# Attention and two MLPs on one core: the attention's steps for all head pairs from one written-out list, masks moved as 16 rows, another order of the first MLP's units

## The chip, the core and the metric

The kernel runs on one core of a Trainium2 chip. The core has TensorE (PE, matmuls into the PSUM banks), VectorE (DVE), ScalarE (ACT), GpSimd (POOL) and SyncE (SP), which issues the DMAs here. Each engine takes its instructions from a list of its own, in order, and waits at an instruction until the semaphores of what it reads or overwrites are there. The metric is the device time of the program in microseconds.

## What is computed

Three layers in a row, in fp32. First an attention in which a query sees only the keys that fall into the same cluster (2 batches, 8 heads, 768 tokens, 64 columns per head, 16 clusters):

```
q_assign = np.argmax(np.einsum('bhsd,hcd->bhsc', q_n, c_n), axis=-1)
k_assign = np.argmax(np.einsum('bhsd,hcd->bhsc', k_n, c_n), axis=-1)
mask = q_assign[:, :, :, None] == k_assign[:, :, None, :]
scores = np.where(mask, scale * np.matmul(q, k.transpose(0, 1, 3, 2)), -1000000000.0)
attn = exp(scores - max(scores)); attn = attn / (sum(attn) + 1e-09)
x = np.matmul(attn, v)                                # then [1536 tokens, 512]
x = ((x @ w1) * (x @ w2)) @ w3 @ w_out                # d_ff 1024
out = (sigmoid(x @ w_gate) * (x @ w_val)) @ w_out2    # d_ff 1536
```

## The kernel before

Every fp32 operand of a product is split into a rounded upper half and the rest (`hi`, `lo`), and a product is three matmuls (`mm3`, lines 65 to 67). The eight matrices of the MLPs arrive as 64-bit words and are converted on the chip (`f64_steps`): a load, and then ScalarE, GpSimd and VectorE in turn.

The attention goes by pairs of heads (`pr`, 0 to 7; four pairs are a batch). A pair has two heads (`e`) of three blocks of 256 queries, so there are 48 blocks `i`, and each block has two score tiles `j`. For a block:

- `scores(j)`: four matmuls into a PSUM tile of `ps_s` (two buffers). The operands `QH`, `KH` hold the 64 upper halves and, in rows 64 and up, the one-hot code of the query's cluster and a penalty for each key, so that the mask is added by the matmul. `QX`, `KX` hold the cross terms.
- `maxima(j)` on VectorE, `exponentials(j)` on ScalarE (which also sums the row).
- `transposes(i, k2)`, three groups of four, into `ps_t` (three buffers); `split_hi` on ScalarE and `split_lo` on VectorE take them out as `ph` and `pl` (for three groups in a pair by way of a copy `pc` and GpSimd, `by_pool`).
- `weighted_v(i, k2)`, three groups of four matmuls into the block's `av` bank (`ps_a`, one buffer), and `take_x(i)`, ScalarE's copy `xa` of that bank.

For the next pair, meanwhile: the load of q and k (`raw`, three buffers), `prep_split` into halves, six SBUF-to-SBUF moves by SP for each head (`prep_scatter`), the products with the centroids (`prep_sims`, on PE, into a tile of `ps_s`), the argmax and the one-hot code (`prep_sum` to `prep_turn`), and the moves of the code into rows 64 to 95 of `QH` and `KH` (`prep_mask`). For the pair before: the moves that join the heads (`join_x`), the inverse row sums by way of DRAM (`turn_sums`, `store_sums`, `spread`), `add_x`, `norm_x` and the split of x for the MLP (`split_x`). The first two pairs of the first MLP's weights are converted in pieces between (`convert`).

In the region `tc.manual_schedule` each engine's list is the order in which the Python code calls the helpers: a loop over the blocks with conditions on the block's place in its pair (lines 503 to 600). A helper issues several instructions, on several engines, at one place.

Behind the attention, the first MLP takes `order` (line 666): units (m, u), m the pair of weight columns, u a third of the tokens. Unit (m, u) is 24 matmuls. The tokens of u = 0 belong to batch 0, those of u = 1 reach into batch 1 and need the last pair's x (its first 512 columns, `FIRST`). There the framework's scheduler sets the order, along the order of the calls.

Of the kernel before, what the change touches and what calls it, by code (L numbers as in the profile page):

```python
# [27 lines left out]
def tile_cluster_attention__then__moe__then__gated_moe(  # L28
# [70 lines left out]
    def f64_steps(src, hi, lo, name, f_engine, lo_engine):  # L99

        n = src.shape[-1]
        raw = ws.tile([128, n, 2], U32, tag="f64", name=f"{name}_f64", bufs=3)
        nc.sync.dma_start(raw.rearrange("p n t -> p (n t)"), src.bitcast(U32))
        low, high = raw[:, :, 0], raw[:, :, 1]
        a = ws.tile([128, n], U32, tag="f64a", name=f"{name}_a", bufs=3)
        af = a.bitcast(F32)
        yield
        nc.scalar.activation(af, high.bitcast(F32), AF.Abs)
        nc.gpsimd.tensor_scalar(out=af, in0=af, scalar1=F64_MAX, scalar2=F64_MIN, op0=ALU.min, op1=ALU.max)
        t = cvp["pool"].tile([128, n], U32, tag="t", name=f"{name}_t", bufs=2) if cvp else a  # L110
        r = a if cvp else low
        yield
        nc.vector.tensor_scalar(out=t, in0=a, scalar1=3, scalar2=0x3FFFFFF8, op0=ALU.logical_shift_left, op1=ALU.bitwise_and)
        nc.scalar.activation(r, low, AF.Copy, scale=2.0 ** -29)
        yield
        nc.vector.scalar_tensor_tensor(out=t, in0=high, scalar=0xC0000000, in1=t, op0=ALU.bitwise_and, op1=ALU.bitwise_or)
        f_engine.tensor_tensor(out=a, in0=t, in1=r, op=ALU.add)
        yield
        nc.scalar.copy(hi, af)  # L119
        lo_engine.tensor_tensor(out=lo, in0=af, in1=hi, op=ALU.subtract)  # L120
# [79 lines left out]
    def load_qk(pr):  # L200
        for w in range(2):
            t = core.tile([128, S], F32, tag="raw", name=f"raw{pr}_{w}", bufs=3)
            nc.sync.dma_start(t, qkT[pr, :, w, :])
            raw[pr, w] = t
# [16 lines left out]
    def prep_split(pr):  # L221
        hl = []
        for w in range(2):
            t = raw.pop((pr, w))
            hi = core.tile([128, S], F32R, tag="hi", name=f"hi{pr}_{w}", bufs=2)
            lo = core.tile([128, S], F32R, tag="lo", name=f"lo{pr}_{w}", bufs=2)
            if w == 0:
                nc.scalar.activation(hi, t, AF.Copy, scale=0.125)
                yield
                nc.vector.scalar_tensor_tensor(out=lo, in0=t, scalar=0.125, in1=hi.bitcast(F32), op0=ALU.mult, op1=ALU.subtract)  # L230
            else:
                split(t, hi, lo, nc.scalar, nc.vector if pr == 0 else nc.gpsimd)
            hl += [hi, lo]
        opnd[pr, "hl"] = hl

    def prep_scatter(pr, e):
        qh, ql, kh, kl = opnd[pr, "hl"]
        r = slice(64 * e, 64 * e + 64)
        QH = core.tile([96, S], F32R, tag="QH", name=f"QH{pr}_{e}", bufs=3)
        KH = core.tile([96, S], F32R, tag="KH", name=f"KH{pr}_{e}", bufs=3)  # L240
        QX = core.tile([128, S], F32R, tag="QX", name=f"QX{pr}_{e}", bufs=3)
        KX = core.tile([128, S], F32R, tag="KX", name=f"KX{pr}_{e}", bufs=3)
        move(QH[0:64], qh[r])
        move(KH[0:64], kh[r])
        move(QX[0:64], qh[r])
        move(QX[64:128], ql[r])
        move(KX[0:64], kl[r])
        move(KX[64:128], kh[r])
        opnd[pr, e] = (QH, KH, QX, KX)

    def prep_sims(pr):


        hp = pr % NP
        qh, ql, kh, kl = opnd[pr, "hl"]
        sp = ps_s.tile([128, 1024], F32, tag="s", name=f"sims{pr}")
        ops = [(0, qh), (1, kh), (0, ql), (1, kl)]
        for c0, c1 in ((0, 512), (512, 768)):
            for i, (w, t) in enumerate(ops):
                nc.tensor.matmul(sp[:, c0:c1], cw[:, hp, w, :], t[:, c0:c1], start=i == 0, stop=i == 3)  # L260
        opnd[pr, "sims"] = sp

    def prep_sum(pr):
# [5 lines left out]
    def prep_add(pr):  # L269
# [5 lines left out]
    def prep_argmax(pr):  # L275
        sm = opnd.pop((pr, "sm"))
        mx = core.tile([128, S // 32], F32, tag="mx", name=f"mx{pr}", bufs=2)
        shape = [128, S // 32, C]
        nc.vector.tensor_reduce(out=mx, in_=sm, axis=AX.X, op=ALU.max)
        nc.vector.tensor_tensor(out=sm, in0=sm, in1=mx.unsqueeze(2).broadcast_to(shape), op=ALU.is_ge)  # L280
        opnd[pr, "top"] = sm

    def prep_code(pr):
        sm = opnd.pop((pr, "top"))
        lead(pr).tensor_tensor(out=sm, in0=sm, in1=dec.unsqueeze(1).broadcast_to([128, S // 32, C]), op=ALU.mult)
        opnd[pr, "code"] = sm
# [35 lines left out]
    def scores(j):  # L322
# [4 lines left out]
        QH, KH, QX, KX = opnd[pr, e]  # L327
# [14 lines left out]
    def exponentials(j):  # L342
# [5 lines left out]
        if at == 0:  # L348
# [14 lines left out]

    def by_pool(i, k2):

        return k2 == 0 and i % 6 in (1, 2, 4)
# [15 lines left out]
    def split_lo(i, k2):  # L382
# [22 lines left out]
    def take_x(i):  # L405
# [3 lines left out]
        if q0 == 0:  # L409
# [5 lines left out]
    def join_x(pr, cols=ALL):  # L415

        if cols.start == 0:
            acc_x[pr, "xb"] = core.tile([128, S], F32, tag="xb", name=f"xb{pr}", bufs=1)
        xa, x1, xb = acc_x[pr, 0], acc_x[pr, 1], acc_x[pr, "xb"]
        move(xb[0:64, cols], xa[64:128, cols])  # L420
        move(xb[64:128, cols], x1[0:64, cols])
        move(xa[64:128, cols], x1[64:128, cols])

    def invert(pr):

        ss = acc_x[pr, "sum"]
        nc.scalar.activation(ss, ss, AF.Copy, bias=1e-9)
        nc.vector.reciprocal(ss, ss)
# [6 lines left out]

    def store_sums(pr):
        rp = acc_x.pop((pr, "rp"))
        rt = core.tile([2 * KT, 128], F32, tag="rt", name=f"rt{pr}", bufs=1)
        nc.vector.tensor_copy(rt, rp)
        nc.sync.dma_start(r_dram[pr], rt)  # L440

    def spread(pr, tag, bufs):

        r = core.tile([128, S], F32, tag=tag, name=f"r{pr}", bufs=bufs)
        for e in range(2):
            row = r_dram[pr, KT * e : KT * e + KT, :].rearrange("t q -> (t q)")
            nc.sync.dma_start(r[64 * e : 64 * e + 64], row.unsqueeze(0).broadcast_to([64, S]))
        acc_x[pr, "r"] = r
# [13 lines left out]


    with tc.issue_after(cw_done.ins):
        for _ in prep_split(0):
            pass
    prep_scatter(0, 0)
    prep_sims(0)
    prep_sum(0)
    prep_add(0)  # L470
# [3 lines left out]
    prep_argmax(0)
    prep_code(0)
    prep_onehot(0)
    prep_turn(0)
    for e in range(2):
        prep_mask(0, e)
# [14 lines left out]
    CONVERT = {}  # L494
    for pr in range(1, NPR - 1):
        for at in ((1, 2, 3), (1, 3, 5))[(pr - 1) % 2]:
            CONVERT[pr, at] = (pr - 1) // 2
    for at in range(6):
        CONVERT[NPR - 1, at] = 3
    with tc.manual_schedule(engines={mybir.EngineType.PE, mybir.EngineType.DVE, mybir.EngineType.Activation, mybir.EngineType.Pool, mybir.EngineType.SP}):  # L500
        for e in range(2):
            prep_v(0, e)
        for i in range(-2, NB + 2):
            pr, at = divmod(i, 6)
            nxt = pr + 1 if 0 <= i and pr + 1 < NPR else None
            later = nxt + 1 if nxt and nxt + 1 < NPR else None
            late = nxt == 1
# [5 lines left out]
            maxima(2 * i + 3)  # L513
            if nxt and at == 1 + late:
# [278 lines left out]
```

## Time and profile before

| | |
|---|---|
| median of 3 runs | 795.5 us (791.53 to 795.8) |
| profiled execution, its time | 796.85 us |
| profiled execution, its span | 795.0 us |
| mean granted TensorE clock | 0.994 |
| TensorE busy | 773.1 us (97%) |
| VectorE, ScalarE, GpSimd busy | 476.8, 395.5, 342.8 us |

The span goes from the first to the last instruction. Busy times of matmuls are modelled: each is shown somewhat longer than the distance to the next, so a short wait between two can be hidden, and a row's idle time is counted from the modelled end. The granted clock is a share of the full 2.4 GHz; 0.50 is the lower of its two levels, 1.2 GHz, and a mean between is a mix of the two.

### The profile page before, as it was taken

Reading aid. Unit: us, or ns where it says so; the run is one execution under the profiler, and the core shown is the slowest. Engines: PE = TensorE matmul, PEld = TensorE weight load, DVE = VectorE, ACT = ScalarE, POOL = GpSimd, SP = SyncE. Lnnn points to the kernel's source line nnn. Section 1 sums busy time; section 2 is a strip of 40 time slices with the busy share of each in tenths; the row PEclk is TensorE's granted clock in tenths of the full one; section 3 lists DMA queues with packets and bytes.
Section 4 is the critical chain, followed back from the end, with each engine's and each line's share of the span. In section 5 each row is a group of like instructions: output and inputs, shape, how many; then the busy total and the mean of one; then the engine's idle time right before and its main releaser. Section 6 shows DMA issues by size and latency. Waiting matters only on the chain.

```text
span 795.0 us, 11161 instructions
## 1 busy us (share of the span) xinstructions
PE 773.1 (97%) x4053; PEld 659.6 (83%) x4053; DVE 476.8 (60%) x703; ACT 395.5 (50%) x747; POOL 342.8 (43%) x354
## 2 busy tenths in 40 slices
PE   8999999999999899999999999999999999999998
PEld 7888988888888688888888888888888888888886
DVE  6799889988977357755655531467502666335222
ACT  3779789888886266654653220444422443023000
POOL 3447777778666365543552110354402443024100
PEclk9899999999999999999999999999999999999999
DMA  8857766666622334533331100123200232000012
GB/s 221 204 155 179 201 178 161 177 182 151 183 77 64 112 133 159 185 133 106 134 105 54 54 0 1 54 79 118 96 26 1 86 126 80 27 0 1 1 67 92
DMA packets 29127, 82.77 MB, mean 104 GB/s; under 512 B 4848, under 2 KB 5136, under 8 KB 29072
## 3 DMA queue, kind: packets, MB, share of 16 engines
q1 hardware_dynamic: 29072, 82.05, 35.1%
q8 instruction: 32, 0.52, 0.3%
q14 instruction: 23, 0.19, 0.1%
HBM read 52.49 MB, written 3.19 MB: 70 GB/s over the span
## 4 chain that ended last, share of the span: by engine, by line
PE 82%; ACT 5%; DMA 4%; DVE 3%; issue 2%; POOL 2%; SPq 2%; ACTq 0%; POOLq 0%; DVEq 0%
PE p L67 20%; PE p L66 20%; PE p L65 20%; PE pt L361 4%; PE av L402 3%; PE av L403 2%; ACT e L351 2%; PE w34p L67 2%; PE w34p L65 2%; PE w34p L66 2%; SPq L62 2%; PE s L330 2%; PE s L332 1%; PE sims L260 1%; DMA xb<-xa 1%
## 5 line engine op out<-in xcount | busy, mean ns | idle before, releaser
L65 PE MATMUL p<-x,wgv 128*128 128x512 f32 x288 | 112.0, 389 | 0.0
L66 PE MATMUL p<-x,wgv 128*128 128x512 f32 x288 | 112.0, 389 | 0.0
L67 PE MATMUL p<-x,wgv 128*128 128x512 f32 x288 | 112.0, 389 | 0.0
L340 DVE TENSOR_REDUCE nm<-s 128x1 f32<-128x768 f32 x96 | 90.5, 944 | 11.4 <-PE s L333 10.8
L351 ACT ACTIVATE e<-s,nm 128x768 f32<-128x768 f32 x96 | 87.2, 909 | 8.8 <-DVE nm L340 6.8
L402 PE MATMUL av<-ph,vx 128*128 128x256 f32 x288 | 80.6, 309 | 10.3 <-ACT xa L411 10.1
L390 DVE TENSOR_TENSOR pl<-pt,ph 128x512 fp32r<-128x512 f32 x120 | 80.3, 684 | 11.4 <-ACT ph L379 10.2
L379 ACT CAST ph<-pt 128x512 fp32r<-128x512 f32 x120 | 69.3, 595 | 25.1 <-PE pt L361 24.3
L361 PE MATMUL pt<-ident,e 128*128 128x128 f32 x576 | 80.3, 276 | 0.7 <-DVE pl L390 0.7
L54 POOL TENSOR_SCALAR u<-ut 128x512 fp32r<-128x512 f32 x36 | 22.4, 622 | 129.3 <-DVE ut L719 129.2
L65 PE MATMUL p<-x,w 128*128 128x512 f32 x192 | 74.9, 391 | 1.9 <-POOL x L54 1.9
L66 PE MATMUL p<-x,w 128*128 128x512 f32 x192 | 75.5, 393 | 0.3 <-POOL x L59 0.3
L67 PE MATMUL p<-x,w 128*128 128x512 f32 x192 | 75.2, 393 | 0.0
L403 PE MATMUL av<-pl,vx 128*128 128x256 f32 x288 | 72.6, 281 | 0.0
L361 PEld LDWEIGHTS pt<-ident,e 128*128 128x128 f32 x576 | 67.8, 143 | 5.6 <-PE pt L361 0.9
L402 PEld LDWEIGHTS av<-ph,vx 128*128 128x128 f32 x288 | 54.3, 188 | 18.4 <-issue 5.8
L66 PEld LDWEIGHTS p<-x,wgv 128*128 128x128 f32 x288 | 54.1, 188 | 11.3
L65 PEld LDWEIGHTS p<-x,wgv 128*128 128x128 f32 x288 | 54.1, 188 | 11.3
L67 PEld LDWEIGHTS p<-x,wgv 128*128 128x128 f32 x288 | 54.1, 188 | 11.1
L719 DVE TENSOR_TENSOR ut<-p,ut 128x512 f32<-128x512 f32 x36 | 24.8, 688 | 62.1 <-PE p L67 61.6
L120 POOL TENSOR_TENSOR w<-w_a,w 128x512 fp32r<-128x512 f32 x32 | 41.7, 1311 | 39.6 <-ACT w L119 39.6
L65 PE MATMUL p<-wo,u 128*128 128x512 f32 x144 | 56.0, 389 | 0.0
(142 smaller groups left out, 1767.3 us busy)
## 6 DMA issues: line engine op xcount, KB each, us to landing
wgv_f<-in_w_gv_dram SPq DMA_DIRECT2D x24, 512.0 KB, 3.3
wo_f<-in_w_out_dram SPq DMA_DIRECT2D x20, 512.0 KB, 4.2
w_f<-in_w_dram SPq DMA_DIRECT2D x16, 512.0 KB, 3.2
w_f<-in_w3T_dram SPq DMA_DIRECT2D x16, 512.0 KB, 3.7
raw<-in_qkT_dram SPq DMA_DIRECT2D x16, 384.0 KB, 3.2
vraw<-in_v_dram SPq DMA_DIRECT2D x8, 384.0 KB, 3.2
QH<-hi SPq DMA_DIRECT2D x16, 192.0 KB, 3.7
KH<-hi SPq DMA_DIRECT2D x16, 192.0 KB, 3.7
```

The lines of the kernel that those rows point to most:

```text
L65: nc.tensor.matmul(ps, whi, xhi, start=start, stop=False)
L66: nc.tensor.matmul(ps, whi, xlo, start=False, stop=False)
L67: nc.tensor.matmul(ps, wlo, xhi, start=False, stop=stop)
L120: lo_engine.tensor_tensor(out=lo, in0=af, in1=hi, op=ALU.subtract)
L340: nc.vector.tensor_reduce(out=nms[j], in_=sps[j][:, 0:S], axis=AX.X, op=ALU.max, negate=True)
L351: nc.scalar.activation(et, sps.pop(j)[:, 0:S], AF.Exp, bias=nms.pop(j), accum_out=acc_x[pr, "sum"][:, at : at + 1])
L361: nc.tensor.transpose(pt[:, kk, 128 * t : 128 * t + 128], exps[2 * i + t][:, k0 : k0 + 128], ident)
L379: nc.scalar.copy(ph, pt)
L390: nc.vector.tensor_tensor(out=pl, in0=src, in1=ph, op=ALU.subtract)
L402: nc.tensor.matmul(avs[i], w, ph[:, kk, :], start=kt == 0, stop=False)
L403: nc.tensor.matmul(avs[i], w, pl[:, kk, :], start=False, stop=kt == KT - 1)
L719: nc.vector.tensor_tensor(out=ut, in0=pv, in1=ut, op=ALU.mult)
```

## The change

The helpers of the attention are cut into single steps, most of them one instruction each (`hi_q`, `lo_q`, `hi_k`, `lo_k`, `scatter(pr, e, n)`, `sims`, `sims_turn`, `top`, `mark`, `code`, `onehot`, `turn_oh`, `penalty`, `mask`, `v_hi`, `v_lo`, `join`, `take_sums`, `half_x`, and more `yield`s in `f64_steps`). A table `PLAN` of 1,352 entries names every step of all eight pairs; the code walks through it and calls each step, so that the table sets the order on all five engines. A block's groups of transposes, its score tiles and the conversions can so stand in any order. The masks are 16 rows (the clusters) and no longer 32, and `QH`, `KH` have 80 rows. In the first MLP the unit (1, 0) becomes the second and (0, 1) the third. The instructions are the same in number (3,969 on PE before and after).

```diff
@@ f64_steps
+        yield
         a = ws.tile([128, n], U32, tag="f64a", name=f"{name}_a", bufs=3)
         af = a.bitcast(F32)
+        nc.scalar.activation(af, high.bitcast(F32), AF.Abs)
         yield
-        nc.scalar.activation(af, high.bitcast(F32), AF.Abs)
         nc.gpsimd.tensor_scalar(out=af, in0=af, scalar1=F64_MAX, scalar2=F64_MIN, op0=ALU.min, op1=ALU.max)
...
@@ the steps of a pair
-    def prep_scatter(pr, e):
-        qh, ql, kh, kl = opnd[pr, "hl"]
-        r = slice(64 * e, 64 * e + 64)
-        QH = core.tile([96, S], F32R, tag="QH", name=f"QH{pr}_{e}", bufs=3)
-        KH = core.tile([96, S], F32R, tag="KH", name=f"KH{pr}_{e}", bufs=3)
...
+    ROWS = {"QH": 80, "KH": 80, "QX": 128, "KX": 128}
+    PIECES = (("QH", 0, "qh"), ("KH", 0, "kh"), ("QX", 0, "qh"), ("QX", 1, "ql"), ("KX", 0, "kl"), ("KX", 1, "kh"))
+
+    def operand(pr, e, name):
+        if (pr, e, name) not in opnd:
+            opnd[pr, e, name] = core.tile([ROWS[name], S], F32R, tag=name, name=f"{name}{pr}_{e}", bufs=3)
+        return opnd[pr, e, name]
+
+    def scatter(pr, e, n):
+        name, half, src = PIECES[n]
+        move(operand(pr, e, name)[64 * half : 64 * half + 64], opnd[pr, src][64 * e : 64 * e + 64])
...
-        if e == 0:
-            nc.gpsimd.tensor_scalar(out=ohT[64:128], in0=ohT[64:128], scalar1=-1.0, scalar2=BIG, op0=ALU.add, op1=ALU.mult)
-        move(QH[64:96], ohT[32 * e : 32 * e + 32])
-        move(KH[64:96], ohT[64 + 32 * e : 96 + 32 * e])
+    def penalty(pr):
+        ohT = opnd[pr, "oh"]
+        nc.gpsimd.tensor_scalar(out=ohT[64:128], in0=ohT[64:128], scalar1=-1.0, scalar2=BIG, op0=ALU.add, op1=ALU.mult)
+
+    def mask(pr, e, w):
+        ohT = opnd[pr, "oh"]
+        dst = operand(pr, e, "QK"[w] + "H")[64 : 64 + C]
+        rows = slice(64 * w + 32 * e, 64 * w + 32 * e + C)
+        if pr:
+            move(dst, ohT[rows])
...
@@ the attention's order
-        for i in range(-2, NB + 2):
-            pr, at = divmod(i, 6)
...
-            scores(2 * i + 3)
-            take_x(i - 2)
-            split_hi(i - 1, 2)
-            transposes(i, 0)
...
+    PLAN = """
+vh:0.0 S:0 M:0 E:0 S:1 lw:2.1 M:1 E:1 S:2 M:2 T:0.2 H:0.2 L:0.2 S:3 T:0.0 E:2 M:3 S:5 H:0.0 L:0.0 T:0.1 vl:0.0 V:0.0 hq:1 E:3 hk:1 vh:0.1 S:4 H:0.1 lq:1
+T:1.1 sc:1.1.0 M:5 T:1.0 M:4 lk:1 E:5 vl:0.1 si:1.0 si:1.1 H:1.1 E:4 L:0.1 T:2.1 S:6 V:0.1 H:2.1 L:1.1 sc:1.0.2 st:1 sc:1.1.2 H:1.0 sa:1 S:7 M:6 mx:1 ge:1
...
+"""
+    steps_of = {
+        "S": scores, "M": maxima, "E": exponentials, "T": transposes, "H": split_hi, "L": split_lo, "P": pool_hi, "V": weighted_v, "X": take_x,
...
+        for item in PLAN.split():
+            name, *at = item.replace(".", " ").replace(":", " ").split()
+            steps_of[name](*map(int, at))
...
@@ the first MLP
-    order = [(0, 0), (0, 1), (1, 0), (0, 2), (1, 1), (1, 2)]
+    order = [(0, 0), (1, 0), (0, 1), (0, 2), (1, 1), (1, 2)]
```

Three places show how the lists change. The first is TensorE's list between the last `av` matmul of block 27 and the first of block 28 (`av27`, `av28`; `s61` is a tile of scores, `pt29_0` the first group of transposes of block 29, a line of dots stands for rows that repeat the pair above). Before:

```order
L403 MATMUL av27_2462<-pl27_2_2439,vx4_1_2183 128x256
L330 MATMUL s61_2501<-KH5_0_2090,QH5_0_2089 128x512
L331 MATMUL s61_2501<-KH5_0_2090,QH5_0_2089 128x256
L332 MATMUL s61_2501<-KX5_0_2092,QX5_0_2091 128x512
L333 MATMUL s61_2501<-KX5_0_2092,QX5_0_2091 128x256
L361 MATMUL pt29_0_2511<-ident_60,e58_2426 128x128
L361 MATMUL pt29_0_2511<-ident_60,e59_2455 128x128
...
L402 MATMUL av28_2528<-ph28_0_2449,vx4_1_2183 128x256
```

And the same place on TensorE in the changed kernel:

```order
L415 MATMUL av27_2442<-pl27_2_2370,vx4_1_2210 128x256
L370 MATMUL pt29_0_2491<-ident_60,e58_2464 128x128
L370 MATMUL pt29_0_2491<-ident_60,e59_2415 128x128
...
L370 MATMUL pt29_1_2498<-ident_60,e58_2464 128x128
L370 MATMUL pt29_1_2498<-ident_60,e59_2415 128x128
...
L339 MATMUL s62_2511<-KH5_0_2221,QH5_0_2402 128x512
L340 MATMUL s62_2511<-KH5_0_2221,QH5_0_2402 128x256
L341 MATMUL s62_2511<-KX5_0_2249,QX5_0_2278 128x512
L342 MATMUL s62_2511<-KX5_0_2249,QX5_0_2278 128x256
L414 MATMUL av28_2528<-ph28_0_2460,vx4_1_2210 128x256
```

Between the two blocks stand two groups of transposes and a tile of scores, where one group and one tile stood.

The second place is SP's list where the masks of pair 6 are moved (`ohT6` is the pair's one-hot code, `QH6_0` and `KH6_0` the operands of its first head, `xa4` the last of the moves that join the heads of pair 4, `r4` the spread of its inverse sums). Before:

```order
L62 DMA xa4_0_2295<-xa4_1_2506 64x768
L62 DMA QH6_0_2539<-ohT6_2809 32x768
L62 DMA KH6_0_2540<-ohT6_2809 32x768
L62 DMA QH6_1_2680<-ohT6_2809 32x768
L62 DMA KH6_1_2681<-ohT6_2809 32x768
L447 DMA r4_2840<-r_dram_65 64x768 x2
```

And on SP in the changed kernel:

```order
L62 DMA xa4_0_2294<-xa4_1_2516 64x768
L62 DMA QH6_0_2727<-ohT6_2819 16x768
L62 DMA KH6_1_2845<-ohT6_2819 16x768
L62 DMA KH6_0_2533<-ohT6_2819 16x768
L210 DMA raw7_1_2930<-in_qkT_dram 128x768
L62 DMA KX6_1_2863<-lo6_1_2538 64x768
```

The first head's second mask now goes third, and the fourth mask move (`QH6_1`) stands some rows further down, behind loads and moves of other pairs.

The third place is TensorE's list where the first MLP begins (`p1_m_u_j` is the product j of unit (m, u), `w12_0` and `w12_1` the first and second pair of weights, `x` the attention's output; a line of dots stands for the rest of a product). Before:

```order
L67 MATMUL p1_0_0_1_3909<-x_150,w12_0_291 128x512
L65 MATMUL p1_0_1_0_3924<-x_150,w12_0_291 128x512
...
L65 MATMUL p1_0_1_1_3937<-x_150,w12_0_291 128x512
...
L65 MATMUL p1_1_0_0_3952<-x_150,w12_1_292 128x512
...
L65 MATMUL p1_0_1_0_3924<-x_150,w12_0_291 128x512
```

And on TensorE in the changed kernel:

```order
L67 MATMUL p1_0_0_1_3909<-x_150,w12_0_291 128x512
L65 MATMUL p1_1_0_0_3924<-x_150,w12_1_292 128x512
...
L65 MATMUL p1_1_0_1_3937<-x_150,w12_1_292 128x512
...
L65 MATMUL p1_0_1_0_3952<-x_150,w12_0_291 128x512
```

Before, unit (0, 1) starts second, runs through three quarters of its two products and the first four matmuls of (1, 0), and its last quarter (the last row, the 47th matmul of the MLP) is the first to need the last pair's x. Now the whole unit (1, 0) stands ahead of (0, 1), and the first matmul that needs this x is the 58th.

## Rows read from the trace of the kernel before

**Rows 1.** The page's first part: busy us, share of the span, instructions.
```profile
span 795.0 us, 11161 instructions
...
PE 773.1 (97%) x4053; PEld 659.6 (83%) x4053; DVE 476.8 (60%) x703; ACT 395.5 (50%) x747; POOL 342.8 (43%) x354
```

**Rows 2.** Busy us by stretch: PE, PEld, DVE, ACT, POOL; clock; DMA share, GB/s.
```profile
17.00:30.30 13.30, 10.79 (x49) 9.28 (x49) 8.13 (x10) 9.96 (x17) 1.82 (x1) 0.74 0.75 206
52.57:81.58 29.01, 27.59 (x203) 25.29 (x202) 26.15 (x39) 25.02 (x54) 19.97 (x19) 1.00 0.72 189
81.58:110.21 28.63, 27.59 (x202) 25.32 (x202) 25.68 (x37) 24.33 (x53) 22.21 (x21) 1.00 0.75 196
264.30:270.73 6.43, 4.23 (x12) 2.86 (x11) 3.61 (x5) 1.38 (x3) 3.17 (x3) 0.73 0.45 150
270.73:453.90 183.17, 183.17 (x810) 151.67 (x809) 108.18 (x168) 96.35 (x161) 81.71 (x89) 1.00 0.33 115
```

**Rows 3.** Timeline of TensorE, two blocks: start, us, operation, idle before and releaser.
```profile
92.05 0.60 PE L361 MATMUL pt<-ident,e 128*128 128x128 f32 x4
93.10 0.35 PE L402 MATMUL av<-ph,vx 128*128 128x256 f32 x1 [0.45 <-ACT xa L411]
...
111.44 0.40 PE L330 MATMUL s<-KH,QH 96*128 96x512 f32 x1
...
115.58 0.40 PE L330 MATMUL s<-KH,QH 96*128 96x512 f32 x1
```

**Rows 4.** Pieces of the chain of waits, in order of time: start, us, what.
```profile
61.13 0.45 PE pt L361 x4
...
100.81 0.89 ACT e L351 x2
101.71 0.27 ACT xa L411
...
110.21 1.39 PE sims L260 x8
```

**Rows 5.** TensorE's waits over the span: for whom, us, times, longest.
```profile
PE av L402 <- ACT xa L411: 10.1, 23, 1.0
```

**Rows 6.** Timeline of TensorE, start of the attention.
```profile
20.16 0.50 PE L330 MATMUL s<-KH,QH 96*128 96x512 f32 x1 [1.49 <-ACT e L351]
...
22.15 0.80 PE L330 MATMUL s<-KH,QH 96*128 96x512 f32 x1 [1.02 <-ACT e L351]
...
28.94 0.40 PE L260 MATMUL sims<-lo,cw 128*128 128x256 f32 x2
```

**Rows 7.** DMA issues by line: count, KB each, median us to landing.
```profile
QH<-hi SPq DMA_DIRECT2D x16, 192.0 KB, 3.7
...
QH<-ohT SPq DMA_DIRECT2D x14, 96.0 KB, 2.1
...
xb<-xa SPq DMA_DIRECT2D x2, 64.0 KB, 2.0
```

**Rows 8.** Timeline of GpSimd and TensorE where the first MLP waits.
```profile
265.70 0.62 POOL L54 TENSOR_SCALAR x<-xa 128x512 fp32r<-128x512 f32 x1
...
266.37 0.74 PE L65 MATMUL p<-x,w 128*128 128x512 f32 x2 [1.91 <-POOL x L54]
...
266.40 1.28 POOL L59 TENSOR_TENSOR x<-xa,x 128x512 fp32r<-128x512 f32 x1
```

**Rows 9.** Timeline of SP and TensorE: a pair's second mask move, its first scores.
```profile
98.76 0.54 SPq L62 DMA_DIRECT2D KH<-ohT  x1
...
103.08 0.40 PE L330 MATMUL s<-KH,QH 96*128 96x512 f32 x1
```

More of the change, by code (lines that the diff above doesn't have):

```diff
@@ L219, in lead @@
         return nc.vector if pr == 0 else nc.gpsimd
[L221 to L234, printed above, removed]
@@ L251, in prep_sims, with hi_q @@
-    def prep_sims(pr):
-        hp = pr % NP
[L255 to L263, printed above, removed]
+    def hi_q(pr):
+        hi = core.tile([128, S], F32R, tag="hi", name=f"hi{pr}_0", bufs=2)
+        nc.scalar.activation(hi, raw[pr, 0], AF.Copy, scale=0.125)
+        opnd[pr, "qh"] = hi
@@ L264, in prep_sum, with sims, sims_turn @@
+    def sims(pr, part):
+        hp = pr % NP
+        if (pr, "sims") not in opnd:
+            opnd[pr, "sims"] = ps_s.tile([128, 1024], F32, tag="s", name=f"sims{pr}")
+        sp = opnd[pr, "sims"]
+        c0, c1 = ((0, 512), (512, 768))[part]
+        for i, (w, t) in enumerate(((0, "qh"), (1, "kh"), (0, "ql"), (1, "kl"))):
+            nc.tensor.matmul(sp[:, c0:c1], cw[:, hp, w, :], opnd[pr, t][:, c0:c1], start=i == 0, stop=i == 3)
+    def sims_turn(pr):
         sp = opnd.pop((pr, "sims"))
@@ L347, in exponentials @@
         at = e * KT + q0 // 128 + j % 2
-        if at == 0:
+        if (pr, "sum") not in acc_x:
             acc_x[pr, "sum"] = core.tile([128, 2 * KT], F32, tag="ss", name=f"ss{pr}", bufs=2)
@@ L461, in split_x, with half_x @@
         split(acc_x[pr, 0][:, cols], x_hl[:, hp, 0, to], x_hl[:, hp, 1, to], *engines)
-    with tc.issue_after(cw_done.ins):
[L465 to L470, printed above, removed]
+    def half_x(pr, half, cols=ALL):
+        b, hp = divmod(pr, NP)
+        to = slice(S * b + cols.start, S * b + cols.stop)
+        hi, lo = x_hl[:, hp, 0, to], x_hl[:, hp, 1, to]
+        xa = acc_x[pr, 0][:, cols]
+        if half == 0:
+            nc.gpsimd.tensor_scalar(out=hi, in0=xa, scalar1=1.0, scalar2=1.0, op0=ALU.mult, op1=ALU.mult)
+        else:
+            nc.gpsimd.tensor_tensor(out=lo, in0=xa, in1=hi, op=ALU.subtract)
+    with tc.issue_after(cw_done.ins):
+        for step in (hi_q, lo_q, hi_k, lo_k):
+            step(0)
+    for n in range(6):
+        scatter(0, 0, n)
+    for part in range(2):
+        sims(0, part)
+    sims_turn(0)
+    sims_add(0)
     warm(72, "warm2")
-    prep_scatter(0, 1)
+    for n in range(6):
+        scatter(0, 1, n)
     load_v(0)
[L474 to L477, printed above, removed]
+    top(0, "mx")
+    mark(0)
+    code(0)
+    top(0, "mc")
+    onehot(0)
+    turn_oh(0)
     for e in range(2):
-        prep_mask(0, e)
+        for w in range(2):
+            mask(0, e, w)
     load_qk(1)
```

287 lines of the change are left out of this document (130 added, 157 removed).

## The prediction

> **What bounds the kernel now.** Read the page first [rows 1]: TensorE is busy 773 of 795 us, VectorE 60% of the time, ScalarE and GpSimd half or less. Then the table by stretches [rows 2]: from 270.73 us to 453.90 us TensorE has no gap at all, and its 810 matmuls take 0.226 us each; the same holds to the end of the program but for the last slices of the page's strip. Nothing in the diff touches that part, so what can be won lies ahead of 270.73 us, in three places: the first 13.30 us of the attention (clock 0.74), its body, and the 6.43 us around the first MLP's second unit (clock 0.73).
>
> For the body, take TensorE's timeline. From 111.44 to 115.58 us one block (two tiles of scores, three groups of four transposes, three groups of four `av` matmuls) runs without a wait: 4.14 us [rows 3]. A pair is six of them, 1.39 us of `sims` and one small transpose (0.11 us, a quarter of the 0.45 for four) [rows 4]: 26.3 us. Two pairs in the middle of the attention take 29.01 and 28.63 us [rows 2]. So each pair loses about 2.5 us on TensorE. VectorE is busy for 26.15 and 25.68 us of the same pairs, ScalarE for 25.02 and 24.33 us: no order can bring a pair far under 26.3 us, and VectorE is as near to that floor as TensorE.
>
> Where the time goes is in the list of TensorE's waits: 10.1 us in 23 waits of the first `av` matmul of a block for ScalarE's copy `xa` [rows 5]. There is one `av` bank (`ps_a`, one buffer); the next block writes it when `take_x` has emptied it. In the block at 92.05 us, four transposes (0.45 us by [rows 4]) are followed by `av` at 93.10 us: 0.6 us lost, though the row shows 0.45, since it counts from the modelled end of the transposes [rows 3]. So the 23 waits are about 14 us. ScalarE is late at them because it works its list in order: before such a copy at 101.71 us two exponentials of 0.89 us stand in the chain of waits [rows 4].
>
> **The change, part by part.**
>
> Start. TensorE waits 1.49 and 1.02 us for the first exponentials and then runs at the low level (1.2 GHz) for a while [rows 6]. The new list puts six tiles of scores, five groups of transposes and one `av` group ahead of pair 1's `sims`; the old one had five and three. The `sims` hang on a chain of other engines (ScalarE's rounding, GpSimd's subtraction) whose place hardly moves, so I let them end at 29.18 us as now (the last pair of their matmuls starts at 28.94 [rows 6]), with half a block more done: 2.1 us won. Bounds: nothing, and 6.0 us (the two waits, 2.5, and 13.30 x 0.26 = 3.5 us of lost clock).
>
> Body. The attention ends at 253.9 us (264.30 less the 46 matmuls of the MLP that run behind it, at 0.226 [rows 2]). From 29.2 us there are 224.7 us, 7.8 pairs; at 2.5 us each 19.5 us can be won at most, and nothing at least. The list changes two things there. First, the work between a block's last `av` matmul and the next block's first. Before, 38 of the 47 gaps hold one tile of scores and one group of transposes, 1.14 us. In the new list 24 gaps hold 1.58 us or more, 13 hold 1.14 to 1.26, and 10 hold 0.87 or less (counted in the order, with 0.71 us for a tile of scores, 0.43 for a group of transposes and 0.47 for an `av` group, which add up to the block's 4.14). Half the gaps get more cover, a fifth get less. Second, each small step of the next pair, which stood behind a whole helper, stands alone between two maxima or two splits. No work goes: VectorE's 26 us and ScalarE's 25 us stay. Between nothing and all I take half, 9.7 us, 1.25 us per pair (27.6 us per pair), by the share of gaps with more cover.
>
> Masks of 16 rows. They are 48 KB where the trace has 96 KB (2.1 us to landing), and 192 KB take 3.7 [rows 7]. A straight line through these two gives 1.3 us, but 64 KB take 2.0, so I take 2.0: 0.1 us earlier, at nothing. If the line held, 0.8 us at each of seven pairs would be 5.6 us at most, and only where a score waits for a mask. The score matmuls contract over 80 rows instead of 96 and stream the same columns: nothing.
>
> The MLP's beginning. Now 46 matmuls run after the attention, the 47th waits 1.91 us for the last pair's rounded `x` from GpSimd (265.70 us, 0.62 us long) [rows 8], and the clock falls. Ten matmuls start between 264.30 and 270.73 us (the row's 12 takes in the two that cross its ends): 6.43 - 10 x 0.226 = 4.2 us lost [rows 2]. With (1, 0) second, 57 matmuls stand ahead of the one that needs this `x`, 11 more: 2.5 us, so it is needed at 266.8 us, when it is there even if it comes no earlier (266.3). Its lower half ends at 267.7 [rows 8] and is asked for at 267.0, a wait of 0.7 us; but in SP's new list two of the three moves that join the heads stand ahead of the wait for the inverse sums, not behind it, so it will come earlier. The second weight pair's last step stands on GpSimd ahead of that `x`, so (1, 0) has its weights. I take 4.2; bounds 2 (the clock falls all the same) and 4.2. That this edit costs nothing hangs on the second pair being converted in time; if it isn't, TensorE stops one unit earlier, with the same loss as now.
>
> Conversions of the first two pairs and everything behind them: as many instructions as before, moved; nothing.
>
> Sum: 2.1 + 9.7 + 4.2 = 16.0 us. The profiled execution took 796.85 us, 1.35 above the median of the runs shown (795.5). So 780.9 against the profile, 779.5 against the median.
>
> **Rivals.**
>
> *One bank.* The waits sit at the single `av` bank, which the change leaves. A gap of 1.14 us plus a wait of 0.62 says that 1.76 us is wanted where it waits. The ten short gaps then lose 0.9 to 1.3 us each (10 us), the 13 middle ones 5 (at today's rate, 23 waits of 0.62 in 38 gaps), the long ones little: about 15, as now. The body wins nothing, 2.1 + 4.2 = 6.3: 789.2 us. For it: the waits are all at this one bank. Against it: the copy is late because exponentials stand ahead of it, which the list moves. The Trainium skill says so too (Perfetto Trace Analysis, Identifying Performance Opportunities): a gap that repeats on the engine that should be full can mean too few buffers for the next tile. The trace agrees as far as the place of the 23 waits goes; by that rule the order would win nothing in the body, 789.2 us.
>
> *All of it.* The body runs at the floor: 19.5 instead of 9.7, 769.7 us. Against it: VectorE would have to be busy for 25.9 of 26.3 us.
>
> *Operands late (slower).* Before, the second mask move of the pair's first head is issued at 98.76 us, and its scores start at 103.08 [rows 9]: 4.3 us, of which landing takes 2.1 [rows 7]. In the new list the TensorE work between the place of the last mask move and that head's first scores is 0.9, 2.3, 0.5, 2.5, 2.5, 0.0 and 0.5 us for pairs 1 to 7, and behind the last of the six other moves (3.7 us to landing) 1.8, 3.2, 0.9, 5.8, 1.3, 9.7 and 3.4. If moves went out where they stand, scores would wait 1.9, 0.5, 2.8, 0, 2.4, 2.1 and 1.6 us: 11.3. A wait of 1.91 us cost 4.2 with the clock at the MLP [rows 2, 8], 2.2 times its length; the four of 1.9 and more would then cost 20.2, and all 22.3: 779.5 + 22.3 = 801.8 us. It decides from about 16 us on, 2.3 us per pair. Against it: the place in the list only orders each queue; SP may issue a move as soon as its source is there.
>
> **Chances.** Forecast (half the body, roughly) 0.50; one bank 0.18; all 0.10; operands late 0.13, some of it without the clock (791); no net change for another reason 0.09. A difference under 0.5% (4 us) can't be told from no change here, so faster means under 791.5 and slower over 799.5. Faster: 0.50 + 0.10 + 0.14 of the bank's 0.18 + 0.02 = 0.76; slower 0.12; same 0.12. The range goes from 770 (all) to 793 (one bank, and a few late operands); about 0.07 lies below and 0.13 above. The forecast's own case lies between 774 and 785.
>
> **What the changed profile would show.** Right: pairs (from `sims` to `sims`) of about 27.6 us, the waits of `av` for `xa` near 5 us in sum as the list of waits counts them, no wait of `p` for GpSimd's `x`, and a clock of 1.00 past the end of the attention. One bank: the same 10 us of waits, in fewer and longer pieces. Late operands: waits of a pair's first scores (`s`) for moves into `QH`, `KH`, `QX` or `KX`, with a lower clock behind them. Wrong start: the first `sims` later than 29 us.

## The result, and the profile after

The changed kernel takes 787.75 us (median of 6 runs, 786.29 to 789.25) beside 794.46 us of the kernel before in the same job: ratio 0.9919, 95% interval 0.9895 to 0.9943, so faster by 6.4 us (4.5 to 8.3). I forecast 779.5; the direction and the range hold, but the gain is less than half of the 16.0 us forecast. A second job with the same kernel gave 788.06 us, ratio 0.9910 (0.9896 to 0.9923).

The profiled execution took 788.63 us, 8.2 less than that of before; the spans differ by 8.2 us too. The head of the page after, to be read beside [rows 1]:

```profile
span 786.9 us, 11193 instructions
PE 768.0 (98%) x4053; PEld 657.5 (84%) x4053; DVE 482.6 (61%) x703; ACT 394.9 (50%) x747; POOL 341.5 (43%) x354
```

TensorE's 4053 and VectorE's 703 instructions are as many as before, yet VectorE is busy longer: 482.6 us beside 476.8. TensorE's list of waits up to 275 us, which answers to [rows 5] (engine, waiting line and its releaser; us in total, times, longest us):

```profile
PE s L339 <- ACT e L360: 3.9, 7, 1.4
PE av L414 <- ACT xa L423: 2.5, 1, 2.5
...
PE pt L370 <- DVE pl L399: 1.9, 3, 0.9
PE pt L370 <- DVE rt L454: 1.5, 2, 1.3
PE sims L267 <- DVE lo L235: 1.3, 1, 1.3
```

The 23 waits of `av` for the copy `xa` (10.1 us) are one of 2.5 us. In their place stand waits for VectorE (1.9 + 1.5 + 1.3 = 4.7 us; before, 0.7) and more for the exponentials. There is no wait of `p` for GpSimd's `x`. The same in two rows of the table by stretches, from the first `sims` of pair 1 to the last `av` matmul, first of before, then of after (us, then busy us and instructions of PE, PEld, DVE, ACT, POOL, granted clock, DMA share, GB/s):

```profile
27.29:254.00 226.71, 215.75 (x1571) 197.39 (x1570) 197.78 (x283) 190.85 (x409) 161.39 (x146) 1.00 0.63 161
```

```profile
27.94:249.20 221.26, 211.09 (x1553) 195.43 (x1554) 202.24 (x281) 188.58 (x405) 162.22 (x148) 1.00 0.65 162
```

The body is 5.45 us shorter, but 2.04 us of that (one tile of scores, two groups of transposes and one `av` group, 0.71 + 2 x 0.43 + 0.47) is work that the new list does ahead of the first `sims`: the body itself won 3.4 us. TensorE's idle time in it hardly fell, from 226.71 - 215.75 = 11.0 us to 10.2. And VectorE, with two instructions fewer in that stretch, is busy for 4.5 us more. That row sent me to VectorE's operations.

**VectorE's steps that grew.** Groups of VectorE's instructions by form, 17 to 250 us, first before, then after (busy us, mean ns of one; idle before):

```profile
L390 DVE TENSOR_TENSOR pl<-pt,ph 128x512 fp32r<-128x512 f32 x118 | 78.9, 684 | 10.1 <-ACT ph L379 9.0 <-POOL pl L59 0.5
L230 DVE SCALAR_TENSOR_TENSOR lo<-raw,hi 128x768 fp32r<-128x768 f32 x7 | 7.5, 1066 | 0.0
...
L280 DVE TENSOR_TENSOR sm<-sm,mx 128x384 f32<-128x384 f32 x7 | 3.9, 557 | 0.2
L293 DVE TENSOR_TENSOR oh<-sm,mc 128x384 f32<-128x384 f32 x7 | 3.9, 557 | 0.2
L279 DVE TENSOR_REDUCE mx<-sm 128x24 f32<-128x384 f32 x7 | 3.8, 544 | 0.2 <-POOL sm L272 0.2
...
L113 DVE TENSOR_SCALAR w_a<-w_a 128x512 uint32<-128x512 uint32 x4 | 1.6, 393 | 0.0
```

```profile
L399 DVE TENSOR_TENSOR pl<-pt,ph 128x512 fp32r<-128x512 f32 x120 | 79.0, 678 | 9.0 <-ACT ph L390 8.4
L235 DVE SCALAR_TENSOR_TENSOR lo<-raw,hi 128x768 fp32r<-128x768 f32 x7 | 9.2, 1320 | 1.4 <-DMA QX<-lo 1.4
...
L288 DVE TENSOR_TENSOR sm<-sm,mx 128x384 f32<-128x384 f32 x7 | 6.0, 859 | 0.1
L295 DVE TENSOR_TENSOR oh<-sm,mc 128x384 f32<-128x384 f32 x7 | 5.7, 815 | 0.1
L114 DVE TENSOR_SCALAR w_a<-w_a 128x512 uint32<-128x512 uint32 x4 | 5.0, 1259 | 0.0
L283 DVE TENSOR_REDUCE mx<-sm 128x24 f32<-128x384 f32 x7 | 3.8, 541 | 0.0
```

Four groups grew by 7 x 254 + 7 x 302 + 7 x 258 + 4 x 866 ns = 9.2 us: three that read two tensors of SBUF (`lo`, the mark `sm`, the one-hot `oh`), and the conversion's shift `w_a`. The shift has one input, but runs in a fast mode: before, it took 0.77 ns a column (393 ns for 512), the mark 1.45 (557 for 384). A fifth group, the conversion's step with two inputs in SBUF, grew by 0.6 us (4 x 142 ns). The reduction `mx` (one input) and `pl` (one of its two in PSUM) kept their length. The timeline of VectorE, GpSimd and TensorE at two of the places (start, length; idle before):

```profile
96.91 1.83 POOL L245 TENSOR_TENSOR lo<-raw,hi 128x768 fp32r<-128x768 f32 x1 [1.70 <-ACT hi L240]
97.33 1.69 DVE L114 TENSOR_SCALAR w_a<-w_a 128x512 uint32<-128x512 uint32 x1
100.64 0.63 PE L370 MATMUL pt<-ident,e 128*128 128x128 f32 x4 [0.94 <-DVE pl L399]
...
197.10 1.84 POOL L488 TENSOR_TENSOR x<-xa,x 128x768 fp32r<-128x768 f32 x1
197.55 1.80 DVE L288 TENSOR_TENSOR sm<-sm,mx 128x384 f32<-128x384 f32 x1
```

GpSimd has begun a step of 1.8 us when VectorE's step starts. VectorE's 0.39 us shift ends at 99.02, 0.28 us after GpSimd's step (98.74); its 0.56 us mark at 199.35, 0.41 after GpSimd's 198.94. They stand still while GpSimd works. In this profile 15 steps of the four groups are stretched, by 10.0 us in all, and each of the 15 began while a GpSimd step was already running; of those that did not begin so, none is. What follows in VectorE's line behind the shift (`nm`, `pl`) makes the transposes wait at 100.64.

**The one wait of 2.5 us** lies at the attention's end. The timeline of GpSimd, ScalarE and TensorE there, and the stretch behind it by windows:

```profile
244.45 1.26 POOL L124 TENSOR_TENSOR w<-w_a,w 128x512 fp32r<-128x512 f32 x1
...
245.74 0.67 ACT L108 ACTIVATE w_a<-w_f 128x512 f32<-128x512 f32 x1 [2.45 <-POOL w L124]
246.31 0.36 ACT L423 COPY xa<-av 128x256 f32<-128x256 f32 x1
...
246.72 0.38 PE L414 MATMUL av<-ph,vx 128*128 128x256 f32 x1 [2.50 <-ACT xa L423]
```

```profile
246.60:250.90 4.30, 4.17 (x17) 3.79 (x18) 2.56 (x5) 2.05 (x5) 1.51 (x2) 0.60 0.53 155
```

The copy stands on ScalarE behind an Abs of a later weight, which waits for a buffer that the last step of conversion `cv:2` gives back, and the new list has that step on GpSimd behind the `nx` and `hx` of pair 6. Behind the wait TensorE ran at a granted 0.60 of its 2.4 GHz for 4.3 us in this execution. The profiles of runs 3 and 7 have the same wait of 2.5 us, and there the clock stayed at 1.00 (240.70 to 245.20 us in run 3, 245.70 to 250.20 in run 7).

### The profile page after: what moved, and what is told of

It is laid out like the page before. It is cut to its first block, busy times and chain, and to the rows that moved or that the text cites. A ratio compares the mean times of both kernels' runs of the same rounds, so it can differ in the third digit from the quotient of the medians.

```text
span 786.9 us, 11193 instructions
## 1 busy us (share of the span) xinstructions
PE 768.0 (98%) x4053; PEld 657.5 (84%) x4053; DVE 482.6 (61%) x703; ACT 394.9 (50%) x747; POOL 341.5 (43%) x354
## 4 chain that ended last, share of the span: by engine, by line
PE 85%; DVE 5%; ACT 2%; issue 2%; POOL 2%; DMA 2%; SPq 1%; POOLq 0%; ACTq 0%; DVEq 0%
PE p L65 21%; PE p L66 21%; PE p L67 21%; PE pt L370 5%; PE av L414 3%; PE av L415 3%; PE s L339 2%; PE w34p L67 2%; PE w34p L65 2%; PE w34p L66 2%; PE s L341 2%; DVE nm L349 2%; DVE pl L399 1%; ACT e L360 1%; DMA KX<-lo 1%
## 5 line engine op out<-in xcount | busy, mean ns | idle before, releaser
L415 PE MATMUL av<-pl,vx 128*128 128x256 f32 x288 | 74.5, 285 | 0.0
L370 PEld LDWEIGHTS pt<-ident,e 128*128 128x128 f32 x576 | 65.8, 141 | 7.1 <-DVE rt L454 1.9
L714 ACT ACTIVATE ut<-p 128x512 f32<-128x512 f32 x36 | 21.3, 592 | 69.6 <-PE p L67 69.6
```

What stands on the lines that cost most here:

```text
L370: nc.tensor.transpose(pt[:, kk, 128 * t : 128 * t + 128], exps[2 * i + t][:, k0 : k0 + 128], ident)
L415: nc.tensor.matmul(avs[i], w, pl[:, kk, :], start=False, stop=kt == KT - 1)
```

## The experiments

Each is compared with the kernel before in its own job; the changed kernel stood at 0.9919 and 0.9910. The times are medians of 4 to 12 executions.

**1. The units' order alone.** In the kernel before, line 666:

```diff
-    order = [(0, 0), (0, 1), (1, 0), (0, 2), (1, 1), (1, 2)]
+    order = [(0, 0), (1, 0), (0, 1), (0, 2), (1, 1), (1, 2)]
```

> The kernel before with one edit: the second weight pair is the first MLP's second unit. By my prediction's step it wins what TensorE lost there, 4.2 us (ratio 0.9947, span near 790.8 us), and the profile shows no wait of p for GpSimd's x and no lower clock between 264 and 271 us. Rival 1: the clock falls all the same, 2 us. Rival 2: the unit order alone wins nothing in the kernel before, because there the rounded x of the last pair comes too late even for 11 more matmuls (it started at 265.70 us); then the changed kernel's gain there came from the new list.

792.91 us, ratio 0.9977 (0.9965 to 0.9988): 1.8 us won; span 792.0. The clock stays at 1.00 where the first MLP begins (262.00 to 272.00 us; 0.83 before), and `p` waits only for the lower half:

```profile
PE p L66 <- POOL x L59: 0.6, 1, 0.6
```

My count for this case was 0.7 us. The order does win by itself, but about my lower bound of 2, not 4.2. (By spans it is 3.0; single profiles of one kernel differ by up to 2 us, below.)

**2. The late conversion.** In the changed kernel's list:

```diff
-... sp:6.0 L:46.0 X:45 ... nx:6 V:46.2 T:47.2 H:47.0 jf:0 hx:6.0 X:46 H:47.2 jf:1 cv:2 sp:7.0 ...
+... sp:6.0 L:46.0 cv:2 X:45 ... nx:6 V:46.2 T:47.2 H:47.0 jf:0 hx:6.0 X:46 H:47.2 jf:1 sp:7.0 ...
```

> The changed kernel with one entry of the list moved: the last step of the weight conversion cv:2 (GpSimd) stands ahead of the sixth pair's nx and hx instead of behind them. Theory A (the one wait of 2.5 us of av for xa at 244 us is ScalarE standing in line behind an Abs that waits for a buffer which that GpSimd step gives back): 2.4 us less, span 784.4 us, and the wait of 2.5 us is gone. Rival (the Abs waits for its data or for another reader): the wait stays, span within 0.5 us of 786.9.

785.1 us, ratio 0.9878 (0.9858 to 0.9898), span 783.1. The Abs and the `av` matmul in its timeline:

```profile
242.52 0.67 ACT L108 ACTIVATE w_a<-w_f 128x512 f32<-128x512 f32 x1 [0.68 <-POOL w L124]
...
244.00 0.39 PE L414 MATMUL av<-ph,vx 128*128 128x256 f32 x1 [0.29 <-ACT xa L423]
```

Theory A holds; 2.9 us (from 0.99145, the mean of the two jobs, to 0.9878, times 794.7), a little over the wait, in line with the lower clock behind it. Of the versions here that compute what the reference asks for this is the fastest.

**3. One input instead of two.** In the changed kernel, the mark and the one-hot of all pairs and `lo` of pairs 1 to 7 get a form of nearly the same length that reads one tensor. It leaves out the marks, the one-hot codes and the lower halves, so runs 3, 4 and 5 measure time only:

```diff
-        nc.vector.scalar_tensor_tensor(out=lo, in0=raw.pop((pr, 0)), scalar=0.125, in1=opnd[pr, "qh"]...)
+        nc.vector.tensor_scalar(out=lo, in0=raw.pop((pr, 0)), scalar1=0.125, ..., op1=ALU.add, accum_out=...)
-        nc.vector.tensor_tensor(out=sm, in0=sm, in1=opnd.pop((pr, "mx")), op=ALU.is_ge)
+        nc.vector.tensor_reduce(out=sm[:, :, 0], in_=oh[:, :, 0:C], axis=AX.X, op=ALU.max)
-        nc.vector.tensor_tensor(out=oh[:, :, 0:C], in0=opnd[pr, "sm"], in1=opnd.pop((pr, "mx")), op=ALU.is_equal)
+        nc.vector.tensor_reduce(out=oh[:, :, 0], in_=opnd[pr, "sm"], axis=AX.X, op=ALU.max)
```

> The changed kernel; three VectorE steps of pairs 1 to 7 (the mark, the one-hot and the lower half of q) are put in a form of about the same length that reads one tensor of SBUF instead of two; the masks and the lower half are then not those of the reference. Theory lock (such a step stands still while GpSimd works; these and four conversion steps took 10.0 us more than their shortest in the changed kernel, 0.8 in the kernel before): the stretched time falls to about 3.5 us, the waits of pt and sims for VectorE go from 4.7 us to 2 or less, and the time falls by 3 to 5 us (span 782 to 784). Theory load (VectorE is full whatever its steps wait for, 26 us of a pair's 26.3): same length of steps, so span within 1 us of 786.9.

783.38 us, ratio 0.9858 (0.9836 to 0.9879), span 780.0: 4.5 us less than the changed kernel by the ratios. The three groups by form, and TensorE's waits for VectorE:

```profile
L238 DVE TENSOR_SCALAR_CACHE_REDUCE lo<-raw 128x768 fp32r<-128x768 f32 x7 | 6.6, 945 | 1.4 <-DMA QX<-lo 1.4
L114 DVE TENSOR_SCALAR w_a<-w_a 128x512 uint32<-128x512 uint32 x4 | 4.0, 1000 | 0.0
L292 DVE TENSOR_REDUCE sm<-oh 128x24 f32<-128x384 f32 x7 | 3.8, 545 | 0.1
L300 DVE TENSOR_REDUCE oh<-sm 128x24 f32<-128x384 f32 x7 | 3.8, 545 | 0.0
```

```profile
PE pt L375 <- DVE pl L404: 1.3, 2, 0.9
PE pt L375 <- DVE rt L459: 0.4, 1, 0.4
PE sims L270 <- DVE lo L238: 0.3, 1, 0.3
```

The three groups are at their short lengths, though 13 of their steps begin while a GpSimd step is running (the longest take 953 ns for `lo` and 554 ns for the others); the shift, which was left, is still at 1000 ns; the 4.7 us of waits are 2.0.

**4. The control: the same replacement in the kernel before.**

> The same three steps put in the form with one input, in the kernel before, as a control: there they were stretched by 0.8 us in sum (two steps). Theory lock: span within 1 us of 795.0. If the third run won its 5 us by something else that the replacement brings (shorter steps, fewer waits for hi), the kernel before wins as much: span 790.

793.46 us, ratio 0.9980 (0.9965 to 0.9995), span 793.2: 1.6 us won, a little more than the lock theory said. Two pairs by windows, beside 29.01 and 28.63 us in [rows 2]:

```profile
51.20:80.18 28.98, 27.52 (x203) 25.23 (x202) 26.03 (x40) 24.91 (x54) 19.69 (x19) 1.00 0.74 190
80.18:108.34 28.16, 27.41 (x204) 25.14 (x203) 25.26 (x38) 24.12 (x53) 20.87 (x19) 1.00 0.72 193
```

The first pair stays as it was. The second gets 0.5 us shorter: it is one of the two whose `lo` stood still in the kernel before (1357 ns instead of 950). The other pairs alternate in the same way, 28.98 and 28.16 us. So in the pairs the replacement wins only where there was a standstill. The control won 1.6 us in all, of which 0.8 was standstill; if it won as much in the new order, at most 1.6 of the 4.5 us of run 3 are something else.

**5. Both costs out**, the edits of 2 and 3 in the changed kernel.

> The edits of the second and the third run together, in the changed kernel (masks and lower half not those of the reference). If the two named costs are what stood between my forecast and the result (2.5 us of the late conversion, 5 to 6 us of VectorE standing still beside GpSimd), they add: span 777 to 779, median 778 to 781, ratio near 0.981. If TensorE's waits only move (theory load), the two together win no more than the third run alone: span 780.

780.3 us, ratio 0.9814 (0.9794 to 0.9834), span 778.4. The two add: 2.9 + 4.5 = 7.4 us apart, 8.0 together (0.99145 to 0.9814). TensorE waits 0.3 us for the copy and 2.1 for VectorE (`pl` 1.2, `lo` 0.5, `rt` 0.4).

**6. Masks of 32 rows** in the changed kernel (`ROWS` 96, moves of 32 rows).

> The changed kernel with masks of 32 rows again (moves of 96 KB, score matmuls over 96 rows). My prediction costs this part at nothing: span within 1 us of 786.9. Rival (late operands: a mask lands 0.8 us later by the line through two sizes, at seven pairs): up to 5.6 us slower, with waits of the scores for moves into QH or KH.

786.66 us, ratio 0.9897 (0.9876 to 0.9919), which can't be told from the changed kernel. Scores wait 1.0 us for the masks in two places. Its span (784.7) is shorter for another reason: some of the standstills of VectorE did not happen in that execution (TensorE waits 2.7 us for VectorE instead of 4.7).

**7. The changed kernel again.**

> The changed kernel itself, for a second profile. If whether VectorE or GpSimd comes first is decided by less than 0.1 us in some places, the list of stretched VectorE steps differs from the first profile's (10.0 us in 15 steps; the copy with 32-row masks had 7.0 in 13), and the span lies between 784 and 787.5 us; if the timing is fixed, the same 15 steps and 786.9.

Span 785.0: VectorE's one-hot of pair 4 did not stand still (0.56 us instead of 1.67), the shift at 172 us by 0.15 instead of 1.07. The first `sims` start at 29.15 us here, at 27.94 in the first profile: from 17.00 to 30.30 us the granted clock was 0.74 here, as in the kernel before, and 1.00 there. So single spans of one kernel differ by up to 2 us, at the start and in the standstills; 787.75 and 788.06 us are the better numbers.

**8. More cover.** In the kernel before, lines 563 to 567:

```diff
-            transposes(i, 2)
...
             weighted_v(i - 1, 2)
+            transposes(i, 2)
```

> The kernel before with one move: the third group of transposes of a block stands behind the last av group of the block before it, not ahead of it. Between two blocks' av matmuls TensorE then has 1.58 us of other work everywhere instead of 1.14. My prediction's step (what covers the copy xa decides; 1.14 + 0.62 = 1.76 us are wanted): of the 23 waits of av for xa (10.1 us as the list of waits counts them, some 14 us as starts of matmuls show) nearly all go, and the time falls by up to 12 us (span 783); what VectorE or ScalarE then can't deliver shows as new waits of pt or s. Rival one bank: the waits move and stay 8 us or more, span 793 to 796. Rival load (VectorE's 26 us with what it waits for set a pair's 28.8 us): the av waits go, as many us of other waits come, span 793 to 796.

793.09 us, ratio 0.9979 (0.9966 to 0.9992). The copy's waits and two pairs by windows:

```profile
PE av L402 <- ACT xa L411: 9.8, 21, 1.0
```

```profile
51.20:80.22 29.02, 27.59 (x205) 25.28 (x203) 26.14 (x38) 25.01 (x55) 19.77 (x18) 1.00 0.72 189
80.22:108.86 28.64, 27.54 (x204) 25.27 (x203) 25.68 (x36) 24.34 (x54) 22.28 (x20) 1.00 0.77 195
```

My cover theory falls: with 0.44 us more work in every gap the waits stay and the pairs are the same to 0.01 us. TensorE only does its transposes later. Counted in the timelines, the copy starts 1.23 us behind the block's last `av` matmul instead of 0.81: the `av` matmuls come earlier and the copy does not, since it stands behind an exponential (45 of 48, as before) whose scores did not come earlier. The 1.7 us that the run wins lie elsewhere: from pair 2's `sims` to pair 7's it takes 144.6 us, the kernel before 144.3.

**9. The same, with the units' order.**

> The kernel before with the third transposes moved as in the run above, and with the second weight pair as the first MLP's second unit. If the two edits act apart: the run above less 2 to 4 us. By the cover theory 780 us, by the load theory 791.

792.11 us, ratio 0.9964 (0.9952 to 0.9976): 1.2 us more than 8.

**10. The copy ahead of the exponential**, in the kernel before:

```diff
-            take_x(i - 2)
...
-            exponentials(2 * i + 4)
             weighted_v(i - 1, 2)
+            take_x(i - 1)
+            exponentials(2 * i + 4)
```

> The kernel before with one step moved on ScalarE alone: the copy xa of a block stands ahead of the exponential of the scores issued just before it, right behind the block's last av matmuls in the list; TensorE's, VectorE's and GpSimd's orders in the attention stay. In the kernel before 45 of 48 copies start with an exponential ahead of them, 0.82 us after the last av matmul on the mean; in the changed kernel 14 of 48 and 0.37 us. Theory line (the 23 waits came from the copy's place behind the exponentials, not from too little other work on TensorE): the waits of av for xa fall from 10.1 us to under 3, pairs from 28.8 us to 27.0 to 27.8, the time by 7 to 12 us (span 783 to 788). Theory load (VectorE's and ScalarE's work sets a pair's 28.8 us): other waits of as many us come, span 793 to 796.

790.79 us, ratio 0.9951 (0.9937 to 0.9965). Its waits:

```profile
PE pt L361 <- DVE pl L390: 5.6, 8, 1.2
...
PE av L403 <- POOL pl L59: 1.4, 4, 0.4
...
PE av L402 <- ACT xa L411: 0.5, 1, 0.5
```

The waits for the copy go, 10.1 to 0.5 us, with TensorE's, VectorE's and GpSimd's work of the attention in the old order: their cause was the copy's place on ScalarE (no copy has an exponential ahead of it any more, and it starts 0.14 us behind the last `av` matmul). But 7.0 us of waits for the split `pl` come (0.7 before), and 3.9 us are won where the theory said 7 to 12. How much of these new waits is standstill (three shifts took 0.59 us too long here) and how much VectorE's load, no run separates.

**11. The same, with the units' order.**

> The same with the second weight pair as the first MLP's second unit: two moves in the kernel before, without the written-out list. Another 2 to 4 us less than the run above: by the theory of the line 779 to 785, below the changed kernel's 786.9 span; by the load theory 790 to 793.

788.84 us, ratio 0.9933 (0.9913 to 0.9953): two small moves win most of what the written-out list wins.

**12. Two banks for `av`**, in the kernel before: `ps_a` two buffers, `ps_t` two instead of three.

> The kernel before with two banks for av and two instead of three for the transposes (there are eight banks, and all are in use). Rival one bank: the waits of av for xa go, and the time falls by up to 12 us unless the third transposing bank was worth as much. Theory line: the waits of av for xa go as well, but then pt waits for VectorE's pl, since a third group of transposes in a block now needs the bank of the first: 5 us or more of such waits, span 790 or more.

810.03 us, ratio 1.0208 (1.0179 to 1.0237). No wait for `xa` is left, but transposes wait for splits (`rp`, the turned row sums, for another 4.4 us):

```profile
PE pt L361 <- DVE pl L390: 17.7, 17, 1.5
```

The bank was not worth its price.

**13. The mark and the one-hot made exactly with one input**, in run 2's kernel: GpSimd subtracts the maximum, and VectorE compares with zero.

> The changed kernel with the conversion step moved as in the second run, and with the mark and the one-hot made exactly, but in two steps: GpSimd subtracts the maximum, VectorE compares with zero, one input in SBUF and the form that also sums. Theory lock: these 14 steps are not stretched any more (2.8 us of stretch in the second run's profile, 4.0 in the changed kernel's), VectorE's waits fall; against that stand 14 more steps of 1.0 us on GpSimd and VectorE standing in line for them. 1 to 3 us less than the second run (span 780 to 782) if the steps on GpSimd come in time, 2 to 6 us more if VectorE waits for them each time.

793.96 us, ratio 0.9984 (0.9971 to 0.9997), 8.4 us slower than run 2 by the ratios. Neither step stands still any more, but TensorE's waits for splits grow to 1.3 us (`av` for VectorE's), 2.6 (`av` for GpSimd's) and 2.9 (`pt`). VectorE waits 2.6 us before its marks and 6.1 us before its one-hot codes for GpSimd's new steps: the 14 steps cost more than the standstill.

## Why the prediction was right in direction and wrong in size

**The terms by the profiles.** With the first `sims`, the end of the last `av` matmul and the end of the span as borders (27.29, 254.02 and 795.0 us before; 27.94, 249.19 and 786.9 in the first profile; 29.15, 248.17 and 785.0 in run 7; 27.32, 241.58 and 778.4 in run 5), and 2.04 us of work moved from the body to the start, the gains are (us):

| term | forecast | first profile | second (run 7) | both costs out (run 5) |
|---|---|---|---|---|
| start | 2.1 | 1.4 | 0.2 | 2.0 |
| body | 9.7 | 3.4 | 5.7 | 10.4 |
| behind the attention | 4.2 | 3.4 | 4.2 | 4.2 |
| sum | 16.0 | 8.2 | 10.0 | 16.6 |

One profile of the kernel before stands behind all of them, 2.4 us above its median, so by medians the sums are smaller: 6.4, 7.2 and 14.8.

**Start (2.1).** Half a block more is done ahead of the first `sims`, as counted. What this wins goes with the clock from 17.00 to 30.30 us: at 1.00 (first profile, runs 2, 3 and 6) the first `sims` start at 27.2 to 27.9 us, at 0.74 (run 7) at 29.15.

**Body (9.7).** This term was mis-sized: 3.4 us, 5.7 in the second profile. Two sentences of mine failed in it. One was that the cover between two `av` groups decides about the copy's waits. It doesn't (run 8); the copy's place on ScalarE does (run 10): 45 of 48 copies had an exponential between the block's last `av` matmul and their own start before, 14 of 48 after (counted in the timelines of the two engines). I had named the exponentials as the reason for the copy's lateness, but sized the term by the cover. By the new place the waits for the copy went more thoroughly than "half", 10.1 us to 2.5. The other was "No work goes: VectorE's 26 us and ScalarE's 25 us stay". VectorE's did not stay: 9.2 us came to it as standstill, because the list cuts the preparing steps apart and starts them while GpSimd works. In the old order GpSimd was idle, had just ended or came second at all but two of these steps. Run 3 with its control 4 puts a price of 2.9 to 4.5 us on three of the four kinds.

The Trainium skill (SBUF — State Buffer, Who interferes with whom) states this as a rule: a VectorE instruction with two inputs in SBUF contends with a GpSimd instruction that reads SBUF, one in a two-port mode with any, and whoever comes second stands still until the other's whole instruction is done; a reduction never contends. The trace agrees (1.80 us for a mark of 0.56, while `mx` stays at 0.54); that the shift runs in such a mode is inferred from its 0.77 ns a column. I did not weigh it: the kernel before shows only 0.8 us of it. But a list that moves such steps past each other was the case for it. That a GpSimd step which only writes SBUF does not contend with one that has two inputs there, as the page says too, no run here shows.

**"Conversions ... moved; nothing".** One was not nothing: `cv:2` behind `nx` and `hx` cost 2.9 us (run 2): a wait of 2.5, and in some executions the low clock behind it.

These two costs, 2.9 and 4.5 us, measured together as 8.0 us (run 5), make up the whole shortfall: 787.75 - 8.0 = 779.75 beside 779.5 forecast. In the table, too, the terms come near their forecasts once both are out. For the body that is partly luck: the cover by which I sized it decided nothing in run 8, and the waits for the copy went to 0.3 us there, where I took half.

**The MLP's beginning (4.2).** Right in mechanism: no wait of `p` for the rounded `x`, no low clock from that place (run 1). The size is open: behind the attention the profiles are 3.4 and 4.2 us shorter, but by medians the order alone is worth 1.8 us (0.9 to 2.8), and in runs 9 and 11 it adds 1.2 and 1.4. I had read the 4.2 from one execution in which the clock fell at that wait; in run 8's profile the wait is longer (2.3 us), and the clock stays at 1.00 (262.00 to 272.00 us). In the changed kernel the last pair's `x` is rounded at 253.96 us, long before it is asked for.

**Masks of 16 rows, nothing:** no difference shows (run 6), within some 3 us.

**The rivals.** *One bank* named the nearest time (789.2), but its mechanism is refuted: with the one bank the 23 waits became one, and in run 10 they went with one move on ScalarE. Run 12 says only that a second bank is not worth a transposing bank. *All of it* was out of reach: even in run 5 the body won 10.4 of the 19.5 us. *Operands late* did not happen: TensorE's list names no move into `QH`, `KH`, `QX` or `KX`. It was nearer than that sounds: the moves of `hi` into `QH` took 6.5 us to landing (median; 3.7 before), in run 6 scores wait 1.0 us for masks, and the step `lo` that makes the `sims` wait 1.3 us had itself waited 1.4 us for a move out of its buffer (`DMA QX<-lo`). My sign "pairs of 27.6 us" was badly chosen: the new list puts the `sims` at other places of a pair, and their distances go from 19.3 to 31.4 us. The sign of a clock at 1.00 past the attention's end failed in the first profile, by the wait of 2.5 us.

## What to carry to other kernels

When steps are reordered, count on each pair of engines what will now run side by side, not only what each has to do: steps of VectorE that read two SBUF tensors (or run in the fast mode, as the shift does) are best put where GpSimd waits. A copy that frees a bank belongs ahead of what its engine does for later blocks; more work on the waiting engine does not help where the copy's own line is late. And for each step that "costs nothing" in its new place, look for the buffer that it gives back and who stands in line for it.

## What the runs showed of the hardware that I had not expected

VectorE's standstill beside GpSimd: a shift of 0.39 us took up to 1.69, a mark of 0.56 up to 1.80, always when a GpSimd step had begun before. Reductions, the form of `lo` that also sums, and steps with their second input in PSUM never grew (541 to 545, 945 and 678 ns on the mean). Whether it happens can change from run to run of the same program (15 such steps in one profile, 13 in another). And the same wait can cost a low clock in one execution and not in the next: the wait of 2.5 us at the end of the attention was followed by 4.3 us at a granted 0.60, on a page whose strip shows 9 everywhere, and by 1.00 in the profiles of runs 3 and 7.
